# A recurrence and a bilinear feed-forward layer on one core: values loaded as 32-bit words, 512-column filling matmuls, sums of logarithms in place, and a new order of all work

## The chip, the cores and the metric

The kernel runs on one core of a Trainium2 chip. The metric is device time in microseconds (us) of one execution. Three executions of the kernel before took 206.62, 208.76 and 208.07 us, median 208.07 us. One further execution was profiled; it took 209.25 us, of which 207.3 us lie between its first and its last recorded instruction (the span).

Names of engines: PE is the matrix engine (PEld its weight loads), DVE the vector engine, ACT the scalar engine, POOL the general engine, SP the one that only issues transfers. Each works through its own list of instructions in order and waits on semaphores.

## The reference

Four sequences with eight heads, 768 steps, 48 elements per head. Each head holds a 48x48 state that decays by `alpha` and takes in an outer product; the result feeds a bilinear layer (3072 rows, 384 wide, 1536 hidden).

```python
for t in range(S):
    state = alpha[:, :, t, :, None] * state + np.einsum('bhd,bhe->bhde', k[:, :, t], v[:, :, t])
    y[:, :, t] = np.einsum('bhd,bhde->bhe', q[:, :, t], state)
x = y.transpose(0, 2, 1, 3).reshape(B * S, H * D)
out = ((x @ w_a) * (x @ w_b)) @ w_out
```

## The kernel before, in words

The steps are cut into six chunks: chunk c holds 256 steps (part c // 2 of the sequence) of two of the four sequences, u = 0 and 1. 128 partitions hold the 256 steps as neighbouring pairs, so each tile of inputs is `[128, 2 (u), 8 (heads), 2 (even and odd step), 48]`.

One chunk goes through two stages.

**Recurrence.** `ln` takes logarithms of alpha (ACT). `l2` adds the two steps of a pair (DVE). `A` (chunk 0, 32-bit matmul) or `H`, `L`, `A2` (chunks 1 to 5: the sum is split in two rounded parts, then two matmuls) multiply by a triangle of ones, which gives cumulative sums over pairs. `le` subtracts the odd step's logarithm to get the sum up to the even step. Four exponentials per u follow (`E`: b for the decay, i for its inverse, 0 for even and 1 for odd steps). `mk` and `mq` multiply keys and queries by them (DVE) into QKp. These are turned by PE and copied back (`C`, `Ce`, chunks 0 and 1) or turned by one transfer per u (`T`, chunks 2 to 5, issued by SP). `v` copies the values into a padded 16-bit tile. `D` makes scores for four heads (u, half), `M` masks them (DVE), `Y` multiplies them by the values, `SB` and `SA` add what the carried state gives, `X` copies the result from PSUM into xT. `K` and `k` bring the state forward; the decay of 64 pairs that they need comes from PE and ACT (`dk`, `de`) or by four small transfers through DRAM (`dec`).

**Feed-forward.** Hidden columns come in 12 blocks of 128. `a f` and `b f` are three matmuls each, either over both u (`*`, 512 columns) or over one (`0` or `1`, 256 columns); `as` copies the first product to SBUF (ACT), `pr` multiplies it by the second (DVE). `o m h` is six matmuls of 384 columns for 128 output rows, `ot` copies them out of PSUM, `st` stores them in two transfers on SP.

`ld` loads an input (chunks 0 and 1: each u by itself), `W` a slice of columns of w_a or w_b, `Wo` a half of w_out; the weights are rounded to 16 bit by the transfer, and so are the values in the kernel before, which takes POOL's queue. `warm n` issues n matmuls on zeros.

Nothing decides the order but a list written out by hand, PROGRAM (lines 17 to 425): each entry is a chunk and operations, issued in that order on the engine that each names. PSUM banks (0 to 7) are written into the list as well, so a matmul into a bank waits for whoever last read it. `gatet u` is a one-element POOL copy that holds POOL's list until the turned keys of u have landed; the next chunk's loads stand behind it.

The tiles la, l2, lh, ll and le exist once each, the input tiles twice.

Of the kernel before, what the change touches and what calls it, by code (L numbers as in the profile page):

```python
# [8 lines left out]
F32 = mybir.dt.float32  # L9
BF16 = mybir.dt.bfloat16  # L10
# [7 lines left out]
0: c1; warm 70 0; cz 0 V; cs 0 V  # L18
0: ld a 0 Y; ld k 0 Y; ld q 0 Y; ld a 1 Y; ld k 1 Y; cs 1 V; ld q 1 Y; gate a 0; ln 0; ld v 0 P; cm 0; cm 1; l2 0 V; A 0 1; warm 48 0; le 0; E 0 b1
0: E 0 i1; cz 1 V; W a 0 256; E 0 i0; W b 0 256; mk 0 V; ln 1; ld v 1 P  # L20
1: ld a 0 P
0: E 0 b0; l2 1 V
1: ld k 0 P
0: mq 0 V; A 1 0
1: ld q 0 P
0: warm 4 1; le 1; E 1 i1
1: ld v 0 P
0: C 0 0 1; dk 6; W a 256 768; E 1 b0; Ce 0 0 V; E 1 i0; W b 256 768; D 0 0 2; E 1 b1; v 0 V; warm 5 4; de; mk 1 V; W a 768 1536; C 0 1 0; K 0 6
0: W b 768 1536; Ce 0 1 S; mq 1 V; warm 11 1
1: ld a 1 P  # L30
0: k 0 0 V; C 1 0 4
1: ld k 1 P
0: M 0 0; SB 0 0
1: ld q 1 P
0: C 1 1 5; Ce 1 0 S
1: ld v 1 P
0: k 0 1 V; D 0 1 2; Ce 1 1 S; Wo 0 6; M 0 1; D 1 0 6; warm 16 4; Wo 6 12; v 1 S; M 1 0
2: ld a * P
0: K 1 4; Y 0; SA 0; k 1 0 V
2: ld k * P  # L40
0: SB 1 6; D 1 1 2; X 0 S; M 1 1
2: ld q * P
1: ln 0
0: a 1 0 0; a 0 0 1
2: ld v * P
0: k 1 1 V; as 1 0; Y 1; SA 1; b 1 0 5; X 1 S; pr 1 0; as 0 0
1: l2 0 V
0: a 5 0 2
1: H 0 S
0: a 3 0 4; as 5 0; a 4 1 5  # L50
1: L 0 V
0: b 0 0 1; as 3 0; a 4 0 6; pr 0 0; a 5 1 7; a 2 0 3; as 4 1; b 5 0 2; b 3 0 0; pr 5 0; b 4 1 4; pr 3 0; as 5 1; b 5 1 2; pr 4 1; as 4 0; b 4 0 7
0: a 2 1 1; as 2 0; pr 4 0; a 1 1 4; pr 5 1; b 2 1 0
1: A2 0 5
0: as 2 1; a 3 1 2
1: le 0; E 0 i1
0: b 3 1 7; b 2 0 6; as 1 1; pr 2 1; a 7 * 3
1: E 0 i0
0: pr 2 0; a 10 * 1; as 3 1
1: mk 0 V; E 0 b1  # L60
0: b 1 1 2; as 10 *; a 6 * 0; pr 3 1; pr 1 1
1: E 0 b0
0: a 0 1 5
1: v 0 V
0: as 7 *; b 11 * 4
1: mq 0 V
0: as 6 *; b 10 * 6; b 7 * 3
1: ln 1
0: pr 10 *; a 11 * 7; pr 7 *; as 0 1; b 6 * 0
1: l2 1 V  # L70
0: as 11 *
1: C 0 0 1
0: pr 6 *
1: H 1 S
0: a 9 * 3
1: Ce 0 0 S; L 1 V
0: b 0 1 2
1: dk 6
0: pr 11 *; as 9 *; pr 0 1
1: D 0 0 4  # L80
0: b 9 * 1
1: de; M 0 0; A2 1 7; C 0 1 6; E 1 i1
0: pr 9 *
1: K 0 2; E 1 b1
0: a 8 * 0
1: k 0 0 V; le 1
0: b 8 * 5
1: k 0 1 V; E 1 b0
0: o 3 0 1; as 8 *
1: mq 1 V; E 1 i0  # L90
0: o 0 0 3; pr 8 *
1: Ce 0 1 S
0: o 2 0 0
1: mk 1 V; SB 0 6; D 0 1 4; C 1 0 2; M 0 1
0: o 0 1 -; o 2 1 -; ot 0 S; o 3 1 -; ot 2 V
1: Ce 1 0 V
0: st 2 Y
1: Y 0; SA 0
0: ot 3 S
1: v 1 V; D 1 0 0  # L100
0: st 3 Y
1: K 1 4; X 0 S; M 1 0; C 1 1 3
2: ln *
1: b 3 0 2; a 1 0 6; Ce 1 1 V; b 11 0 1; a 3 0 0; k 1 0 V
0: o 1 0 7
1: as 3 0
2: l2 * V
1: as 1 0; b 1 0 0; k 1 1 V
0: o 1 1 -
2: H * S  # L110
1: pr 3 0; a 0 0 5; pr 1 0
0: ot 1 S
1: a 11 0 4
2: L * V
1: b 0 0 2; as 0 0; a 5 0 0; as 11 0; a 8 0 3; pr 0 0; as 5 0; SB 1 6; D 1 1 4; pr 11 0; as 8 0; a 4 0 0; M 1 1
2: A2 1 2
1: as 4 0
2: A2 0 1; E 1 i1
1: b 4 0 3; a 2 0 0
2: le 1; E 0 b1  # L120
1: b 5 0 4
2: le 0; E 1 b1
1: b 8 0 5; Y 1; SA 1
2: E 1 i0
1: pr 4 0
2: dec
1: pr 8 0
2: E 0 b0
1: pr 5 0; a 6 0 3; X 1 S
2: mk 1 V  # L130
1: a 7 0 2; a 10 0 5; as 2 0; b 11 1 7
2: mq 0 V; E 0 i1
1: b 2 0 4
0: st 1 Y
1: b 6 0 0; as 7 0; b 7 0 1; as 6 0; pr 2 0; a 9 0 6
2: E 1 b0
1: pr 7 0; a 2 1 3
0: st 0 Y
1: a 0 1 2; pr 6 0; as 10 0; b 10 0 4
2: mq 1 V  # L140
1: as 2 1; b 2 1 0; as 0 1; b 0 1 5
2: v 1 S
1: a 9 1 1; pr 10 0
2: T 1
1: b 9 1 2; pr 0 1; a 5 1 3; as 9 1; pr 2 1; a 4 1 4
2: E 0 i0
1: b 4 1 1; pr 9 1; as 4 1; b 5 1 5
2: mk 0 V
1: a 11 1 0; as 9 0; b 9 0 4; as 5 1; a 3 1 2; pr 4 1
2: T 0  # L150
1: b 3 1 6; pr 9 0; as 3 1; a 1 1 1; pr 5 1; a 8 1 3; as 11 1; b 1 1 4; pr 3 1; as 1 1; a 10 1 0; pr 11 1; as 8 1; b 8 1 6; pr 1 1
2: v 0 S; gatet 1; D 1 0 2
3: ld a * P
1: pr 8 1; a 7 1 1
2: M 1 0
1: as 10 1
2: K * 6
1: as 7 1
3: ld k * P
1: b 6 1 5  # L160
2: k * 0 V
1: a 6 1 3; b 7 1 4
3: ld q * P
1: as 6 1
2: D 0 0 0
1: o 3 0 2
2: k * 1 V
3: ld v * P
1: pr 7 1; b 10 1 6; o 2 0 3; pr 6 1; pr 10 1
2: M 0 0; SB 1 4; D 1 1 6  # L170
1: o 2 1 -
3: ln *
2: M 1 1
1: o 1 0 1; ot 2 S
3: l2 * V
2: Y 1; SA 1
3: H * V
1: o 1 1 -
2: X 1 S
3: L * V  # L180
2: SB 0 6
1: ot 1 S
2: D 0 1 4
1: o 0 0 3
2: M 0 1
1: st 1 Y
3: A2 0 0; A2 1 1; E 0 b1
2: Y 0; SA 0
3: le 1; E 0 i1; le 0; E 1 b1
1: o 3 1 -  # L190
2: X 0 V
3: E 0 i0; dec; E 1 i1
1: o 0 1 -
3: v 0 V; E 1 i0; mk 0 V; E 0 b0
2: a 4 * 7
3: E 1 b0; mq 0 V
2: a 3 * 0
1: st 2 Y
2: a 0 * 5; as 3 *
3: mq 1 V  # L200
2: b 3 * 6
3: T 0
2: as 4 *
3: mk 1 V
2: a 6 * 1
3: v 1 S
2: b 4 * 4; pr 3 *
1: ot 0 S
2: b 0 * 7; as 6 *
1: st 0 Y  # L210
2: pr 4 *; a 1 * 3; as 0 *; b 6 * 6
1: ot 3 S
2: pr 0 *
3: T 1
2: as 1 *; a 9 * 5
1: st 3 Y
2: pr 6 *; b 1 * 2; as 9 *
3: D 0 0 0
2: pr 1 *
3: K * 6; M 0 0  # L220
2: b 11 * 5; b 2 * 2
3: k * 0 V
2: a 11 * 1
3: gatet 1
2: a 2 * 0
4: ld a * P
2: as 11 *
3: k * 1 V
2: b 9 * 4; as 2 *
4: ld k * P  # L230
2: b 7 * 3; pr 9 *; a 7 * 1; pr 11 *
4: ld q * P
2: a 8 * 6; as 7 *; pr 2 *; a 5 * 0
4: ld v * P
2: as 8 *; pr 7 *
3: D 1 0 4
2: as 5 *; a 10 * 7
3: M 1 0
2: b 8 * 1; as 10 *; b 5 * 2; pr 8 *
4: ln *  # L240
3: SB 1 6
2: pr 5 *
3: D 1 1 4
2: b 10 * 0
3: M 1 1
2: o 0 0 2
4: l2 * V
2: o 3 0 3; pr 10 *
4: H * S
3: Y 1; SA 1  # L250
4: L * V
3: SB 0 4; D 0 1 0; X 1 S
2: o 0 1 -
3: M 0 1
4: A2 0 7
2: o 1 0 6; ot 0 V
4: E 0 b1; le 0
2: st 0 Y
3: Y 0; SA 0
4: E 0 b0  # L260
2: o 3 1 -
3: X 0 S
4: E 0 i1; A2 1 0
3: b 11 * 4
4: E 0 i0; le 1
3: a 0 * 2
2: ot 3 V
4: E 1 b0
3: a 11 * 5
4: mq 0 V  # L270
2: o 2 0 1
3: as 11 *
4: mk 0 V
3: as 0 *; b 0 * 3
4: T 0; E 1 i0
2: o 2 1 -
3: pr 0 *
4: E 1 i1; v 0 S; mk 1 V
2: o 1 1 -
4: E 1 b1  # L280
3: a 7 * 5
2: ot 2 S
4: mq 1 V
3: b 7 * 3
4: v 1 S
2: st 2 Y
3: pr 11 *; a 8 * 0
2: ot 1 S
3: a 5 * 1
4: T 1  # L290
3: as 7 *; b 8 * 2
4: dec
3: pr 7 *; as 5 *
4: D 0 0 6
3: a 3 * 5
4: M 0 0
3: a 2 * 1; as 3 *; b 5 * 3
2: st 1 Y
3: as 8 *; b 2 * 7; pr 5 *
2: st 3 Y  # L300
3: b 3 * 4; pr 8 *; as 2 *
4: gatet 1
5: ld a * P
3: a 1 * 6; pr 3 *; a 4 * 5; pr 2 *; as 1 *
5: ld k * P
3: b 1 * 4; as 4 *; b 4 * 2; pr 1 *
5: ld q * P
4: K * 6
3: pr 4 *; a 6 * 3
5: ld v * P  # L310
4: k * 0 V
3: b 6 * 1; as 6 *
4: D 1 0 4
3: pr 6 *
4: SB 1 2; D 1 1 6
3: a 10 * 0
4: M 1 0
3: a 9 * 1; as 10 *
4: M 1 1
3: b 10 * 5; as 9 *; b 9 * 4  # L320
5: ln *
3: o 2 0 1; pr 9 *; pr 10 *
4: SB 0 6; Y 1; SA 1
5: l2 * V
4: D 0 1 4
3: o 0 0 0
4: X 1 S; M 0 1
5: H * S
3: o 0 1 -
5: L * V  # L330
4: Y 0; SA 0
5: A2 1 2
4: X 0 S
3: o 2 1 -
5: le 1; E 1 i1
3: ot 0 V
4: a 4 * 7
5: E 1 i0; E 1 b0
4: b 6 * 6
5: mk 1 V; E 1 b1; A2 0 0  # L340
4: a 6 * 5
3: ot 2 V
5: E 0 b1
4: b 3 * 3
5: dec
4: as 6 *; a 3 * 1; as 4 *; pr 6 *; a 1 * 5; as 3 *
5: mq 1 V
4: b 4 * 6; as 1 *
5: le 0
4: b 1 * 1  # L350
5: T 1; E 0 i1
4: pr 4 *; a 7 * 2
5: E 0 i0
4: pr 3 *; a 0 * 5; as 7 *
5: mk 0 V
3: o 1 0 6
5: E 0 b0; v 0 S
4: pr 1 *; b 0 * 7; as 0 *
3: o 1 1 -
5: v 1 V; mq 0 V  # L360
4: a 5 * 1
3: ot 1 S
4: pr 0 *
5: T 0; K * 4
4: as 5 *
# [48 lines left out]
5: as 9 *; b 2 * 2; as 6 *; b 9 * 6; a 2 * 7; pr 9 *
4: o 2 0 4
# [13 lines left out]
def kernel(  # L429
# [11 lines left out]
    nc = tc.nc  # L441
# [479 lines left out]
```

## Time and profile before

| | before |
|---|---|
| median of three executions | 208.07 us |
| profiled execution, span | 209.25 us, 207.3 us |
| PE busy, matmuls | 192.6 us, 2702 |
| DVE, ACT, POOL busy | 139.9, 101.2, 38.0 us |
| first feed-forward matmul | 22.27 us |
| last matmul's start, last instruction | 202.66 us, 207.3 us |
| transfers | 29.42 MB, mean 142 GB/s |
| instruction queue q8 | 21 packets, 0.34 MB |

Times count from the span's start. A row of the page's fifth part gives a group of equal instructions: count, total busy time, mean duration, then the idle time of the engine before them and what ended it. Matmuls overlap in the pipeline, so a mean duration (379 ns for 512 columns) is longer than the distance between two starts. That distance, read from the start times in the trace where PE runs without a break, is 0.216 us for 512 columns, 0.109 us for 256, 0.163 us for 384 and 0.056 us for 128.

The page's second part cuts the span into 40 slices of 5.18 us; a digit is the busy share in tenths, and PEclk is the granted clock of PE. The trace also records transfers by queue; queue q8 brings PE's instructions in packets of 16,384 bytes, 256 instructions of 64 bytes.

### The profile page before, as it was taken

Reading aid. Unit: us, or ns where it says so; the run is one execution under the profiler, and the core shown is the slowest. Engines: PE = TensorE matmul, PEld = TensorE weight load, DVE = VectorE, ACT = ScalarE, POOL = GpSimd, SP = SyncE. Lnnn points to the kernel's source line nnn. Section 1 sums busy time; section 2 is a strip of 40 time slices with the busy share of each in tenths; the row PEclk is TensorE's granted clock in tenths of the full one; section 3 lists DMA queues with packets and bytes.
Section 4 is the critical chain, followed back from the end, with each engine's and each line's share of the span. In section 5 each row is a group of like instructions: output and inputs, shape, how many; then the busy total and the mean of one; then the engine's idle time right before and its main releaser. Section 6 shows DMA issues by size and latency. Waiting matters only on the chain.

```text
span 207.3 us, 6249 instructions
## 1 busy us (share of the span) xinstructions
PE 192.6 (93%) x2702; PEld 121.6 (59%) x2718; DVE 139.9 (67%) x223; ACT 101.2 (49%) x192; POOL 38.0 (18%) x54
## 2 busy tenths in 40 slices
PE   8988499999999989999998899999999999999991
PEld 8867378575778866564545554456545554454560
DVE  5799435887599979579885766698597755423530
ACT  3456344874378850567342576535683344332200
POOL 3896636000000027000080000530000000000000
PEclk9999859999999999999999999999999999999998
DMA  6999999999310697997959919699457200004155
GB/s 163 239 238 246 207 243 232 225 276 215 55 39 4 110 173 198 257 123 141 179 141 263 152 33 196 72 280 263 41 83 145 61 3 0 0 0 112 38 120 112
DMA packets 52587, 29.42 MB, mean 142 GB/s; under 512 B 42760, under 2 KB 49672, under 8 KB 52560
## 3 DMA queue, kind: packets, MB, share of 16 engines
q0 software_dynamic: 19552, 17.70, 45.5%
q1 hardware_dynamic: 33008, 11.33, 28.1%
q8 instruction: 21, 0.34, 0.6%
q14 instruction: 6, 0.05, 0.1%
HBM read 25.98 MB, written 4.74 MB: 148 GB/s over the span
## 4 chain that ended last, share of the span: by engine, by line
PE 53%; issue 24%; DMA 9%; DVE 6%; ACT 4%; POOL 2%; POOLq 0%; ACTq 0%; DVEq 0%
PE psum L789 28%; PE psum L812 15%; DMA a_t<-in_alpha_dram 7%; PE psum L738 4%; DMA kqT<-QKp 2%; ACT la L553 1%; DVE l L559 1%; PE psum L722 1%; PE psum L693 1%; ACT kqT L660 1%; PE psum L574 1%; PE psum L596 1%; DVE S L518 1%; DVE vx L513 1%; DVE m L727 1%
## 5 line engine op out<-in xcount | busy, mean ns | idle before, releaser
L789 PE MATMUL psum<-xT,wa_t 128*128 128x512 bf16 (+1 forms) x262 | 57.2, 344 | 1.3 <-ACT xT L773 0.6
L789 PE MATMUL psum<-xT,wb_t 128*128 128x512 bf16 (+1 forms) x262 | 56.4, 338 | 0.6 <-issue 0.5
L812 PE MATMUL psum<-wo_t,prod 128*128 128x384 bf16 x288 | 51.5, 326 | 0.1
L812 PEld LDWEIGHTS <-prod 128*128 128x128 bf16 x288 | 27.2, 98 | 19.3 <-issue 0.3
L789 PEld LDWEIGHTS <-wa_t 128*128 128x128 bf16 x270 | 26.2, 101 | 20.4 <-issue 0.9
L789 PEld LDWEIGHTS <-wb_t 128*128 128x128 bf16 x270 | 25.8, 99 | 19.9 <-issue 0.3
L727 DVE TENSOR_TENSOR m<-psum,mask 128x1024 bf16<-128x1024 f32 x24 | 29.0, 1220 | 7.9 <-PE psum L722 7.7
L839 POOL CAST go<-kqT 1x1 f32<-1x1 bf16 x3 | 0.5, 173 | 83.9 <-DMA kqT<-QKp 83.9
L773 ACT ACTIVATE xT<-psum 128x768 bf16<-128x768 f32 x11 | 8.9, 808 | 14.4 <-PE psum L738 14.3
L817 ACT ACTIVATE ot<-psum 128x384 f32<-128x384 f32 x13 | 6.4, 492 | 18.2 <-PE psum L812 18.2
L553 ACT ACTIVATE la<-a_t 128x768 f32<-128x768 f32 (+1 forms) x8 | 9.3, 1165 | 11.6 <-DMA a_t<-in_alpha_dram 11.6
L738 PE MATMUL psum<-m,vx 64*64 64x128 bf16 x576 | 10.9, 221 | 2.8 <-issue 2.5
L722 PE MATMUL psum<-kqT 64*64 64x128 bf16 x384 | 10.3, 219 | 2.7 <-DVE prod L802 1.7
L738 PEld LDWEIGHTS <-vx 64*64 64x64 bf16 x576 | 8.9, 109 | 6.1 <-issue 6.1
L570 PE MATMUL psum<-wz 128*128 128x128 bf16 x154 | 11.2, 238 | 1.0 <-DVE one L493 1.0
L614 DVE TENSOR_TENSOR QKp<-k_t,invb 128x768 bf16<-128x768 f32 x12 | 11.4, 953 | 0.9 <-ACT invb L610 0.9
L570 PEld LDWEIGHTS <-wz 128*128 128x128 bf16 x154 | 10.3, 108 | 1.9 <-DVE one L493 1.0
L614 DVE TENSOR_TENSOR QKp<-q_t,beta 128x768 bf16<-128x768 f32 x12 | 11.3, 951 | 0.0
L722 PEld LDWEIGHTS <-kqT 64*64 64x64 bf16 x384 | 7.2, 106 | 5.3 <-issue 3.8
L819 DVE COPY ot<-psum 128x384 f32<-128x384 f32 x11 | 6.0, 553 | 6.0 <-PE psum L812 6.0
L601 DVE TENSOR_TENSOR le<-psum,la 128x384 f32<-128x384 f32 x12 | 6.5, 553 | 5.0 <-PE psum L596 3.7
L559 DVE TENSOR_TENSOR l<-la 128x384 f32<-128x384 f32 (+1 forms) x8 | 6.0, 746 | 4.7 <-ACT la L553 4.7
(244 smaller groups left out, 261.3 us busy)
## 6 DMA issues: line engine op xcount, KB each, us to landing
out_dram<-ot SPq DMA_DIRECT2D x48, 96.0 KB, 2.2
a_t<-in_alpha_dram POOLq DMA_DIRECT2D x4, 768.0 KB, 7.8
k_t<-in_k_dram POOLq DMA_DIRECT2D x4, 768.0 KB, 9.7
q_t<-in_q_dram POOLq DMA_DIRECT2D x4, 768.0 KB, 11.4
v_t<-in_v_dram POOLq DMA_DIRECT2D x4, 384.0 KB, 12.4
wo_t<-in_moe_w_out_dram POOLq DMA_DIRECT2D x2, 576.0 KB, 16.0
a_t<-in_alpha_dram SPq DMA_DIRECT2D x2, 384.0 KB
k_t<-in_k_dram SPq DMA_DIRECT2D x2, 384.0 KB, 6.9
```

Of the source, the lines that this page charges most:

```text
L553: nc.scalar.activation(out=ch.la[:, us].rearrange("p b h r d -> p (b h r d)"), in_=ch.a[:, us].rearrange("p b h r d -> p (b h r d)"), func ...
L559: eng.tensor_add(ch.l2[:, us].rearrange("p b h d -> p (b h) d"), x[:, :, 0, :], x[:, :, 1, :])
L570: nc.tensor.matmul(w[:, :C], lhsT=wz, rhs=wz, start=True, stop=True)
L601: nc.vector.tensor_sub(ch.le[:, u], ch.pf[u].rearrange("p (h d) -> p h d", h=H), ch.la[:, u, :, 1, :])
L614: eng.tensor_mul(QKp[ch.c % 2][:, u, j, :, :, :D], src[:, u].rearrange("p h r d -> p r h d"), by[:, :, u])
L722: nc.tensor.matmul(s2[g * HC:(g + 1) * HC, r, p, rk, :], lhsT=ch.kqT[u][rs, 1, rk, 2 * h + p, g * HC:(g + 1) * HC], rhs=queriesT(ch, u, 2 ...
L727: nc.vector.tensor_mul(m.rearrange("p r a k s -> p (r a) (k s)"), ch.s2[u, h].rearrange("p r a k s -> p (r a) (k s)"), maskn(4))
L738: nc.tensor.matmul(y[c * DP:(c + 1) * DP, g, j // 2 * C:(j // 2 + 1) * C], lhsT=lhsT, rhs=rhs, start=(g, c) not in begun, stop=False, skip ...
L773: nc.scalar.activation(out=o_, in_=i_, func=AF.Copy)
L789: nc.tensor.matmul(p, lhsT=(wa_t, wb_t)[w][:, kk, f * 128:(f + 1) * 128], rhs=ch.xT[:, kk, us, :], start=(kk == 0), stop=(kk == KT - 1))
L812: nc.tensor.matmul(op, lhsT=ch.prod[:, f, m * C:(m + 1) * C], rhs=wo_t[:, f, :], start=(f == 0), stop=(f == NFF - 1))
L817: nc.scalar.activation(out=ot, in_=ch.pf["o", m], func=AF.Copy)
```

## The change

Values stay 32-bit words when they are loaded, so that a load of values may stand on SP's queue; the copy `v` does the rounding. Filling matmuls have 512 columns instead of 128, and there are 37 of them instead of 154 (17 instead of 70 in the first group). Weights come in slices of 256, 768 and 512 columns instead of 256, 512 and 768. The tiles l2 and le are gone: from chunk 1 on the sums of pairs overwrite the even half of la, and `le` later overwrites them in the same place; chunk 0 uses lh and ll for them. Chunk 1's decay goes through DRAM instead of PE. The clearing of the state tiles moves from DVE to POOL. All loads and all operations of PROGRAM stand in a new order, with other banks and in places other engines; chunk 0 makes four of its twelve hidden blocks in halves instead of six.

```diff
-0: c1; warm 70 0; cz 0 V; cs 0 V
-0: ld a 0 Y; ld k 0 Y; ld q 0 Y; ld a 1 Y; ld k 1 Y; cs 1 V; ld q 1 Y; gate a 0; ln 0; ld v 0 P; cm 0; cm 1; l2 0 V; A 0 1; warm 48 0; le 0; E 0 b1
-0: E 0 i1; cz 1 V; W a 0 256; E 0 i0; W b 0 256; mk 0 V; ln 1; ld v 1 P
+0: c1; warm 17 0; cs 0 P; cz 0 V
+0: ld a 0 Y; ld a 1 Y; ld v 0 Y; ld k 0 Y; cm 0; cm 1; ln 0; l2 0 V; ld q 0 P; ln 1; A 0 1; ld k 1 P; warm 3 0; ld q 1 P; l2 1 V; E 0 i1; cs 1 P
+0: E 0 b1; le 0; A 1 7; E 0 b0; dk 0; le 1; E 1 b1; ld v 1 P; v 0 V; E 0 i0; warm 6 2
 1: ld a 0 P
-0: E 0 b0; l2 1 V
+0: E 1 i0; W b 0 256; mk 0 V; E 1 i1; de; W a 0 256; mq 0 V; E 1 b0; K 0 2; warm 2 4
+1: ld a 1 P
+0: C 0 0 0; mk 1 V; W a 256 1024; warm 4 1; Ce 0 0 S; W b 256 1024; k 0 0 V; mq 1 V; W b 1024 1536; D 0 0 6; C 0 1 4; W a 1024 1536; k 0 1 V
+0: C 1 0 5; v 1 S
+1: ld q 0 P
+0: M 0 0; warm 2 0
 1: ld k 0 P
...
+0: Ce 1 0 S; K 1 0
+1: ld k 1 P
+0: warm 1 2; k 1 0 V; Ce 0 1 S
+1: ld q 1 P
+0: D 1 0 6; k 1 1 V; C 1 1 3; Wo 0 6; M 1 0; SB 0 4; Ce 1 1 S; D 0 1 0
 1: ld v 0 P
...
+0: warm 2 2; Wo 6 12
+1: ln 0
+0: M 0 1; SB 1 6; D 1 1 2
 1: ld v 1 P
...
+0: M 1 1
 2: ld a * P
...
+0: Y 0; SA 0
 2: ld k * P
...
+0: X 0 S
+1: l2 0 V
+0: Y 1; SA 1
+1: H 0 S
+0: a 1 0 5
 2: ld q * P
-1: ln 0
-0: a 1 0 0; a 0 0 1
+0: X 1 V
+1: ln 1
+0: b 1 0 3; a 0 0 0; b 0 0 1
+1: L 0 V
 2: ld v * P
...
-    wz = cst.tile([C, C], BF16, name="wz")
+    wz = cst.tile([C, 512], BF16, name="wz")
...
-            setattr(ch, what, ld.tile([C, 2, H, 2, D], BF16 if what == "v" else F32, name=what + "_t"))
+            setattr(ch, what, ld.tile([C, 2, H, 2, D], F32, name=what + "_t"))
...
+    def part(ch, name, dtype):
+        if not hasattr(ch, name):
+            setattr(ch, name, wk.tile([C, 2, H, D], dtype, name=name, bufs=1))
+        return getattr(ch, name)
+
+    def sums(ch):
+
+        return part(ch, "lh", F32) if ch.c == 0 else ch.la[:, :, :, 0, :]
+
     def pairs(ch, us, eng):
-        if not hasattr(ch, "l2"):
-            ch.l2 = wk.tile([C, 2, H, D], F32, name="l2", bufs=1)
         x = ch.la[:, us].rearrange("p b h r d -> p (b h) r d")
-        eng.tensor_add(ch.l2[:, us].rearrange("p b h d -> p (b h) d"), x[:, :, 0, :], x[:, :, 1, :])
+        eng.tensor_add(sums(ch)[:, us].rearrange("p b h d -> p (b h) d"), x[:, :, 0, :], x[:, :, 1, :])
...
-            nc.tensor.matmul(w[:, :C], lhsT=wz, rhs=wz, start=True, stop=True)
+            nc.tensor.matmul(w, lhsT=wz[:, :C], rhs=wz, start=True, stop=True)
...
+    def evens(ch):
+        return part(ch, "ll", F32) if ch.c == 0 else ch.la[:, :, :, 0, :]
+
     def even(ch, u):
-        if not hasattr(ch, "le"):
-            ch.le = wk.tile([C, 2, H, D], F32, name="le", bufs=1)
-        nc.vector.tensor_sub(ch.le[:, u], ch.pf[u].rearrange("p (h d) -> p h d", h=H), ch.la[:, u, :, 1, :])
+        nc.vector.tensor_sub(evens(ch)[:, u], ch.pf[u].rearrange("p (h d) -> p h d", h=H), ch.la[:, u, :, 1, :])
```

`high`, `low`, `cum`, `expo` and `decay_pe` read the sums and the even parts through the new helpers and do the same arithmetic. The lists of chunks 1 to 5 are rewritten throughout. Of the old list the prediction also uses this place (`gatet 1` stands some lines ahead of it):

```
4: ln *
3: SB 1 6
2: pr 5 *
3: D 1 1 4
2: b 10 * 0
3: M 1 1
2: o 0 0 2
4: l2 * V
2: o 3 0 3; pr 10 *
...
3: SB 0 4; D 0 1 0; X 1 S
```

In the new list the same steps of chunks 3 and 4 read `3: D 1 0 6; K * 2` to `4: ln *`, `4: l2 * V`, `3: SB 0 6; D 0 1 4`, with more matmuls of chunk 2 between `gatet` and `l2`; and chunk 1 has `E 1 i1; dec` where the old list has `dk 6` and `de`.

## The prediction

> **What bounds the kernel now.** I read the slices of the page first. The second part of the page, rows PE, POOL, clock and transfers:
>
> ```profile
> PE   8988499999999989999998899999999999999991
> ...
> POOL 3896636000000027000080000530000000000000
> PEclk9999859999999999999999999999999999999998
> DMA  6999999999310697997959919699457200004155
> ```
>
> PE is full almost everywhere from the sixth slice (25.9 us) on. The weak place is the fifth and sixth: a 4 in PE, then an 8 and a 5 in its clock. The stretches 18 to 31.6 us by themselves (columns: length, busy time and instructions of PE, PEld, DVE, ACT, POOL, then granted clock, share of transfers, GB/s):
>
> ```profile
> 18.00:21.40 3.40, 2.73 (x138) 2.46 (x128) 2.67 (x4) 1.37 (x2) 1.78 (x2) 1.00 1.37 214
> 21.40:24.80 3.40, 1.54 (x46) 1.05 (x35) 1.85 (x3) 1.81 (x3) 1.95 (x4) 1.00 1.25 208
> 24.80:28.20 3.40, 2.13 (x34) 1.65 (x35) 0.10 (x1) 0.92 (x2) 1.47 (x2) 0.50 1.17 209
> 28.20:31.60 3.40, 3.40 (x18) 2.35 (x16) 1.77 (x4) 1.62 (x5) 1.17 (x1) 0.50 1.12 272
> ```
>
> After a stretch with PE 45% busy the clock is granted at half for two stretches, and comes back after one that was full. The chain of waits names what emptied it (start, length, what):
>
> ```profile
> 19.70 0.45 issue
> 20.15 0.34 PE psum L693 x19
> ...
> 23.08 0.51 PE psum L738 x25
> 23.59 2.48 issue
> 26.07 1.17 PE psum L738 x28
> 27.24 5.22 PE psum L789 x27
> ```
>
> Two gaps wait for nothing that the profile shows. Counting PE's instructions in program order (each 32-bit matmul is four), the first gap stands before instruction 704 and the second before 960, 256 apart, which is one packet of queue q8. That queue's packets start at 10.75, 17.56, 23.75 and 29.65 us, and PE resumes 1.3 to 1.4 us after the second and third end (18.82 to 20.15, 24.70 to 26.07). I take both gaps as PE out of instructions: it used 256 (short 64-row matmuls) faster than a busy transfer system brought them, about 6 us from one block's use to the next one's arrival (20.15 to 26.07).
>
> [...]
>
> **Part by part.** *Start of the feed-forward.* Before: first matmul of it 22.27 us, and by 32.46 us 36 matmuls of 256 columns (6 before the gap, the others mostly at half clock). After, from rows of this trace: a load of 0.39 MB lands every 1.5 us on SP's queue (alpha 4.64, then 6.14, 7.65, 9.15), so alpha u1, values u0, keys u0 land at 6.1, 7.7, 9.2. POOL first clears state tiles. POOL fills of that size aren't in the trace: at least 0.3 us (its 64x256 fill), at most 1.7 us by the slope from 64 to 256 elements (145 to 320 ns); I take 2.5 us for the pair, the slope, because the list has them unpacked. Its 8 mask steps take 2.6 us, so queries u0 are issued at 7.0 and then keys and queries u1; 3 us to the first packet (issue 8.99, packets 11.8 for weights) and 1.5 us each give landings of 11.9, 13.4, 14.9. A second clearing delays values u1 to a landing near 17. From there by rows: `mq` 11.9, 0.95 us; `C 0 0`; `mq` of u1 at 14.9; `v 1` on ACT 17.1 to 17.95 (845 ns); `K 1`; then `Ce 1 0`, `Ce 0 1`, `Ce 1 1` of 1.02 us each to 21; `M 1 0`, `M 0 1`, `M 1 1` of 1.22 us from 19.5 to 23.2; `Y 0`, `Y 1` of 0.9 us. Without a gap the feed-forward would start at 24.4. The new list reaches it after 771 instructions instead of 897 (37 filling matmuls, not 154), so the block limit at 960 lies after it; only 704 lies in a fast stretch, inside `Y 1`. Its block is asked for when 448 is crossed, just before `C 1 1` near 18.2, and 6 us later is 24.2 against 23.5 when it is wanted: a gap of 0.7 us. Start 25.2, with no recurrence of chunk 0 left. 36 matmuls at 0.109 us end at 29.1 instead of 32.46: **-3.3 us** if the clock stays. Each microsecond by which values u1 land later moves it one to one.
>
> *Weights.* They land by the trace's rates (1.0 us for 256 columns, 2.9 for 768, 1.9 for 512, behind those loads) at 20 to 21, 25.4, 28.3, 30.2, 32.1 us. `a 5` wants the second at 26.5, `b 2 1` the third at 29.3, `b 11` the fourth at 32.5: cover of about 1 us, nothing added. If it goes, PE waits one to one.
>
> *Values as words.* A half of the values took 0.9 us of transfers (landings 21.54 and 22.46), alpha 1.5: +0.6 each, 2.4 us over four halves, before chunk 2's alpha, which I put at 50 us against its use (`ln`) at 53. Hidden with 3 us. On ACT the copy has 845 ns for 16-bit values and I change nothing; on DVE it lies between 351 ns (16-bit row) and 957 ns (128x768 cast from PSUM), four copies, at most 2.4 us of an engine 67% busy: 0.
>
> [...]
>
> *Sums in place.* DVE's sum of 384 elements takes 537 ns, of 768 954 ns; the same work with another stride. New wait: `ln` of the next chunk has to follow the exponentials that read the even part. In the list they are at least 9 us earlier. Price 0; if the strided access were slower by as much as the even exponential is against the odd (518 to 488 ns), 40 such steps cost 1.2 us of ACT and DVE, not of PE.
>
> *Chunk 1's decay.* PE loses 64 records: they took from 43.46 to 44.20, **-0.7 us**. The four transfers on SP stand 10 us ahead of `k`, behind nothing but stores' list.
>
> *Halves.* 24 halves become 12 wholes: 24 x 0.109 = 2.62 against 12 x 0.216 = 2.59. 0. Moving `X`, `ot`, clearing between DVE and ACT: both below 70%, 0; `X` on DVE is 957 against 808 ns, at most 0.15 us on the path each time.
>
> *Chunks 2 to 5.* Here PE waited at 75.2, 86.2, 88.7 and 112.9 us, 0.8, 0.5, 0.5 and 1.9 us. The last, in the timeline (start, length, engine, line, operation, idle before):
>
> ```profile
> 103.12 0.17 POOL L839 CAST go<-kqT 1x1 f32<-1x1 bf16 x1 [21.65 <-DMA kqT<-QKp]
> ...
> 111.74 1.48 ACT L553 ACTIVATE la<-a_t 128x1536 f32<-128x1536 f32 x1 [3.59 <-DMA a_t<-in_alpha_dram]
> ...
> 113.25 0.96 DVE L559 TENSOR_TENSOR l<-la 128x768 f32<-128x768 f32 x1 [2.52 <-ACT la L553]
> ...
> 114.13 0.68 DVE L802 TENSOR_TENSOR prod<-as__2165,psum 128x512 bf16<-128x512 bf16 x1
> ...
> 114.86 0.42 PE L722 MATMUL psum<-kqT 64*64 64x128 bf16 x16 [1.71 <-DVE prod L802]
> ```
>
> DVE sits on the pair sum until alpha has landed behind the gate; the product behind it holds PE's bank. Adding PE's work by the distances in the table, from gate to pair sum: 7.5, 8.4, 10.2 us before (chunks 3, 4, 5), 6.4, 9.9, 8.9 after. From a turn to its first use, chunk 2: 4.6 before (it waited 0.8), 5.6 after. So chunk 4 gains about 1.5, chunk 2 0.8, chunk 3 loses about 1.1: -1.2 on balance, of which I take half, **-0.6**, since banks and DVE's neighbours changed too. Ends: -3.8 (all four gone) to +6 (three such waits of 2 us more).
>
> *End.* The last `o`, `ot` and `st` are the same kind: 0.
>
> Sum: 209.25 - 3.3 - 0.7 - 0.6 = 204.65, so **204.7 us**. The profiled execution lies 1.2 us above the median 208.07; the four times shown spread over 2.6 us, about what the half clock costs (5.6 us of work at half, 2.8 us), so the runs may differ in it.
>
> **Rivals.** *Half clock again.* The new list has fewer fillers late: between 14.5 and 17.9 PE has one `D` (0.42 us), two `C` (0.61 each) and two fillers (0.43), 2.1 of 3.4 us or 60%. If the clock is halved as the feed-forward starts, up to 2.8 us go: 207.5. For: 63% at half clock did not bring it back. Against: 80% kept it. 0.25.
>
> *The fetch gap stays whole* (the change doesn't do what it seems to): `Y 1` waits 2 us more, 206.7. 0.07.
>
> *Slower: DVE stuck on alpha.* The mechanism just shown, in the three pair sums after a gate. For: 6.4 us in chunk 3 against 0.2 + 0.5 + 7.2 for gate, issue and landing plus 1.5 for the logarithms, 9.4 us. Loads of words add to the queue. With 2 us for each of three chunks, and 0.7 of the start's gain lost to values u1: 204.7 + 6 + 0.7 = 211.4. It decides once alpha lands over 10 us after its issue instead of 7.2 to 7.6. Against: turns come earlier than before. 0.23.
>
> **Numbers.** Forecast 204.7 with 0.45 (203 to 206). About 1% is what a measurement can tell from no change: 206.0 to 210.1. The first rival is within it, the second too. Chances: faster 0.50, same 0.26, slower 0.24. Range 202.3 to 210.9: low end with all four waits gone and half a microsecond less clearing, high end into the slower rival.
>
> **What will show it.** The first feed-forward matmul at 24.4 to 26 us; at most one gap without cause, before PE instruction 704, under 1 us; full clock from 26 us; alpha of chunk 2 landed by 51 us; no DVE wait over 2.5 us on logarithms. Wrong if values u1 land after 18 us, if the clock is half past 28 us, or if PE waits in chunks 2 to 4 sum to more than 4 us.

## The result: 237 us instead of 208

The changed kernel takes 237.07 us (median of four executions, 234.51 to 239.48); the kernel before takes 208.41 us beside it (four, 206.62 to 209.17). The ratio is 1.130, 95% interval 1.116 to 1.145; it goes by the two faster executions of the changed kernel alone (234.51 and 236.06), and the profiled one is one of the two slower. The forecast was 204.7 us with a range up to 210.9: wrong, and on the other side.

The profiled execution of the changed kernel took 239.48 us, its span is 236.7 us. From the first and second part of its page:

```profile
span 236.7 us, 5851 instructions
...
PE   7968899920999998999100299999999999999992
...
PEclk9997999995699999999955589999999999999999
DMA  7999999996021799749999700849905656102105
```

A slice is now 5.92 us. The 4 that PE had in its fifth slice before is gone, but PE has two holes that were not there: a 2 and a 0 (47 to 59 us), and 1 0 0 2 (112 to 136 us). Within each hole the clock falls to half, and it stays there from 52.6 to 62.9 us and from 117.5 to 138.0 us. PE works again from 59.6 and from 134.6 us, so only some 3.3 us of work behind each hole run at half clock: an estimate of 1.7 us lost each time. The view of waits (engine and line, what they wait for, total us, times, longest) names both:

```profile
PE psum L734 <- DMA kqT<-QKp: 21.4, 1, 21.4
...
DVE Sm L719 <- DMA bl<-row: 11.1, 1, 11.1
...
PE psum L750 <- DVE Sm L719: 10.5, 1, 10.5
```

Each is one single wait. Chunk 1's carried-state matmuls (L750) wait for `k`, which waits for `bl`, the decay that now comes through DRAM. Chunk 3's scores (L734) wait for `T 0`, the turn of its keys and queries. Neither transfer is issued late. Before, all transfers of the same kinds landed soon after their issue. The views by tile of the kernel before give, for `bl` and then for the turns:

```profile
DMA to landing us min/median/max: 2.0/2.4/2.7
...
DMA to landing us min/median/max: 4.3/4.3/4.4
```

The first place in the timeline of the changed kernel (start, length, engine, line, operation, idle before):

```profile
34.11 1.15 POOL L553 DMA_DIRECT2D a_t<-in_alpha_dram  x1 [0.46 <-DMA k_t<-in_k_dram]
34.68 0.59 SPq L631 DMA_DIRECT2D row<-beta  x2
...
38.36 1.15 POOL L553 DMA_DIRECT2D v_t<-in_v_dram  x1
39.51 0.91 SPq L634 DMA_DIRECT2D bl<-row  x2
...
59.19 0.36 DVE L719 TENSOR_TENSOR Sm<-psum,bl 128x192 bf16<-128x192 f32 x1 [11.11 <-DMA bl<-row]
...
59.60 0.53 PE L750 MATMUL psum<-kqT,Sm 64*64 64x128 bf16 x6 [10.48 <-DVE Sm L719]
```

`bl` is issued in two transfers, at 39.51 and 39.88; the second lands 19.2 us after its issue. Between issue and landing chunk 2's four loads (issued 34.11 to 39.5) are on the way. `bl` consists of 1536 packets of four bytes; the loads' packets mostly have 4224 bytes and take 252 ns each. From 44 to 54 us the records show 672 of the former and 567 of the latter, near one for one, and the small ones speed up when the large ones thin out (483 against 35 in 56 to 58 us). A four-byte packet itself takes 13 ns, which makes 20 us for 1536 one after the other and 1.2 us spread over the page's 16 engines. That `bl` spends the rest of its 19.2 us waiting behind large packets is an estimate from these counts. The last of the small ones starts at 58.5 us, the last packet of the loads at 58.3. The prediction had not weighed such a mixture.

The second place:

```profile
100.84 1.79 SPq L677 DMA_TRANSPOSE kqT<-QKp  x1
102.74 1.14 SPq L631 DMA_DIRECT2D row<-beta  x2
105.24 0.17 POOL L851 CAST go<-kqT 1x1 f32<-1x1 bf16 x1 [17.08 <-DMA kqT<-QKp]
105.39 0.90 SPq L634 DMA_DIRECT2D bl<-row  x2
105.88 1.16 POOL L553 DMA_DIRECT2D a_t<-in_alpha_dram  x1 [0.47 <-ACT ot L829]
106.39 13.35 SPq L677 DMA_TRANSPOSE kqT<-QKp  x1
...
134.59 0.64 PE L734 MATMUL psum<-kqT 64*64 64x128 bf16 x16 [21.40 <-DMA kqT<-QKp]
```

The new list has chunk 3's turns in the order `T 1; dec; ... T 0`, then `gatet 1`. The gate names the turn of u 1, which is the first of the two. So the gate opens at 105.24, chunk 4's loads start at 105.88, and the second turn is issued at 106.39, after them. The first turn of the same chunk took 4.3 us. The second stands in the chain of waits (start, length, what) of the kernel before with the first of these lines, in that of the changed kernel with the second:

```profile
98.58 4.42 DMA kqT<-QKp
...
106.39 28.15 DMA kqT<-QKp
```

Its 2048 packets of 256 bytes took 73 ns in the mean instead of 21. Here the mixture is not one for one: from 109 to 134 us there are 729 packets of the loads beside the 2048. So the account of the first place does not carry over as it stands; why the turn is slow among loads is not shown, only that it is.

**Where the time went.** The table takes the moment at which PE has done a given amount of its work (all matmuls but the fillers, counted in PE time at full clock, 168 us in all; read from the starts of the weight loads, which the trace holds without gaps) and gives the distance to the kernel before in us. Rows below "changed" are the experiments. Each row is one profiled execution; up to the feed-forward they are all one program, and still its first matmul came at 25.3 to 26.9 us.

| work done, us of PE (kernel before is there at) | 26 (49.7) | 32 (56.6) | 74 (102.4) | 80 (109.1) | 164 (197.8) |
|---|---|---|---|---|---|
| changed | -3.9 | +8.2 | +8.0 | +31.1 | +29.7 |
| decay on PE again | -1.9 | -1.7 | -1.7 | +19.9 | +19.8 |
| gate on the last turn | -2.6 | +9.5 | +9.7 | +15.1 | +15.3 |
| loads held behind `bl` | -0.3 | -0.4 | -0.9 | +20.0 | +18.2 |
| both repairs | -2.2 | -1.9 | -0.7 | +3.5 | +5.1 |
| both, alpha ahead of the gates | -2.6 | -2.4 | -3.4 | -3.7 | -1.9 |

The changed kernel is 3.9 us ahead when chunk 0's work is well under way (the forecast had 3.3). Then it loses 12.1 us at the decay and 23.1 us at the turn, and nothing more.

### The profile page after: what moved, and what is told of

It reads as the page before. It is cut to its first block, busy times and chain, and to the rows that moved or that the text cites. A ratio compares the mean times of both kernels' runs of the same rounds, so it can differ in the third digit from the quotient of the medians.

```text
span 236.7 us, 5851 instructions
## 1 busy us (share of the span) xinstructions
PE 192.5 (81%) x2504; PEld 113.7 (48%) x2525; DVE 138.2 (58%) x212; ACT 103.6 (44%) x193; POOL 43.9 (19%) x59
## 4 chain that ended last, share of the span: by engine, by line
PE 40%; DMA 26%; issue 21%; POOL 9%; ACT 1%; DVE 0%; POOLq 0%; ACTq 0%
PE psum L801 20%; PE psum L824 14%; DMA kqT<-QKp 14%; DMA q_t<-in_q_dram 7%; DMA a_t<-in_alpha_dram 6%; PE psum L750 3%; POOL S L526 1%; POOL q_t L553 1%; PE psum L734 1%; POOL k_t L553 1%; POOL wa_t L536 1%; POOL wb_t L536 1%; PE psum L607 1%; POOL v_t L553 1%; POOL a_t L553 1%
## 5 line engine op out<-in xcount | busy, mean ns | idle before, releaser
L801 PE MATMUL psum<-xT,wa_t 128*128 128x512 bf16 (+1 forms) x256 | 56.3, 343 | 0.9 <-ACT as__1451 L807 0.5
L824 PE MATMUL psum<-wo_t,prod 128*128 128x384 bf16 x288 | 52.8, 331 | 1.0 <-ACT ot L829 0.9
L801 PEld LDWEIGHTS <-wa_t 128*128 128x128 bf16 x264 | 25.2, 99 | 21.2 <-issue 2.7
L801 PEld LDWEIGHTS <-wb_t 128*128 128x128 bf16 x264 | 25.1, 98 | 20.8 <-issue 1.3
L734 PE MATMUL psum<-kqT 64*64 64x128 bf16 x384 | 11.6, 234 | 22.3 <-DMA kqT<-QKp 21.4
L829 ACT ACTIVATE ot<-psum 128x384 f32<-128x384 f32 x18 | 8.4, 487 | 27.7 <-PE psum L824 27.6
L734 PEld LDWEIGHTS <-kqT 64*64 64x64 bf16 x384 | 8.0, 114 | 25.4 <-DMA kqT<-QKp 21.9
L750 PE MATMUL psum<-kqT,Sm 64*64 64x128 bf16 x144 | 8.7, 227 | 10.5 <-DVE Sm L719 10.5
L750 PEld LDWEIGHTS <-Sm 64*64 64x64 bf16 x144 | 5.3, 110 | 15.0 <-DVE Sm L719 10.9
L585 PE MATMUL psum<-wz 128*128 128x512 bf16 x34 | 10.9, 457 | 1.4 <-DVE one L501 1.2
L750 PE MATMUL psum<-m,vx 64*64 64x128 bf16 x576 | 10.5, 218 | 1.2 <-issue 0.6
L750 PEld LDWEIGHTS <-vx 64*64 64x64 bf16 x576 | 8.7, 107 | 3.5 <-issue 3.5
L719 DVE TENSOR_TENSOR Sm<-psum,bl 128x192 bf16<-128x192 f32 x4 | 1.4, 356 | 13.4 <-DMA bl<-row 11.1
L785 ACT ACTIVATE xT<-psum 128x768 bf16<-128x768 f32 x8 | 6.5, 807 | 4.6 <-PE psum L750 4.6
```

The lines of the kernel that those rows point to most:

```text
L585: nc.tensor.matmul(w, lhsT=wz[:, :C], rhs=wz, start=True, stop=True)
L734: nc.tensor.matmul(s2[g * HC:(g + 1) * HC, r, p, rk, :], lhsT=ch.kqT[u][rs, 1, rk, 2 * h + p, g * HC:(g + 1) * HC], rhs=queriesT(ch, u, 2 ...
L750: nc.tensor.matmul(y[c * DP:(c + 1) * DP, g, j // 2 * C:(j // 2 + 1) * C], lhsT=lhsT, rhs=rhs, start=(g, c) not in begun, stop=False, skip ...
L785: nc.scalar.activation(out=o_, in_=i_, func=AF.Copy)
L801: nc.tensor.matmul(p, lhsT=(wa_t, wb_t)[w][:, kk, f * 128:(f + 1) * 128], rhs=ch.xT[:, kk, us, :], start=(kk == 0), stop=(kk == KT - 1))
L824: nc.tensor.matmul(op, lhsT=ch.prod[:, f, m * C:(m + 1) * C], rhs=wo_t[:, f, :], start=(f == 0), stop=(f == NFF - 1))
```

## Experiments

Line numbers move by a few from kernel to kernel. "Before" beside each group is the old kernel on the same chip: 209.28 us (median of 7; the first four runs), 209.48 (13; `gateb`, the gate in the old list, and alpha ahead in both kernels) and 209.27 (17; the rest). Runs of different groups are best compared by their ratios to it.

**1. Undo each suspect alone, then both.** The theory is two separate crossings, that is, transfers of small packets that are on the way at the same time as loads; the rival for each is that the new order of feed-forward work holds the loss.

Decay on PE again (`dk`, `de` in place of `dec`):

```diff
-1: le 0
+1: dk 4; le 0
...
-0: cz 1 V; as 6 *; b 2 1 6
+0: cz 1 V
+1: de
+0: as 6 *; b 2 1 6
...
-1: E 1 i1; dec
+1: E 1 i1
```

> The changed kernel, with chunk 1's decay made by PE and ACT again (as in the kernel before) instead of four small transfers through DRAM. Theory (the small transfers crossed chunk 2's loads): the wait of 10.5 us in chunk 1 goes, with the half clock after it (1.6 us of work), and PE gets 0.7 us of its own back: 237 - 11.4, so 225 to 226 us; the wait of 21 us in chunk 3 stays. Rival (chunk 1's state was late for another reason, the sums in place or the late values): the wait stays and the time is 237 to 238.

Measured 229.66 us (ratio 1.095, 1.086 to 1.105). The hole at 49 to 60 us is gone and the other is untouched (table). It came out some 4 us above the expectation. Half of that is there by 49.7 us, where the kernel is 1.9 us ahead instead of 3.9: the banks that the decay holds make a feed-forward group wait 1.40 us, and PE's gap at the start lasted 1.15 us instead of 0.64 (part 5). The other half is not accounted for.

Gate on the last turn:

```diff
-3: gatet 1
+3: gatet 0
```

> The changed kernel with one word changed: in chunk 3 the gate waits for the turned keys of u 0, the turn that is issued last, not of u 1. Theory (the last turn crossed chunk 4's loads): it lands in 4.3 to 4.6 us again, the wait of 21.4 us and 1.7 us of half clock go, chunk 4's alpha comes 5 us later and costs up to 2 us: 214 to 216 us. Rival (the turn was slow by itself or waited for the decay's transfers ahead of it on SP's queue): it still takes over 20 us, and the time is 236 or more.

Measured 223.92 us (1.068, 1.060 to 1.076). One digit gives back 13 us, 8 us less than expected. The same turn, still behind the decay's transfers on SP's list but ahead of the loads, is quick again in the chain of waits:

```profile
108.02 5.94 DMA kqT<-QKp
```

So it was not slow by itself or by the decay ahead of it. Of the 23.1 us at this place 5.4 are left (table, from +9.7 to +15.1): all loads now start later, at 114.73, and alpha is late.

Both:

> The changed kernel with both repairs (chunk 1's decay by PE, chunk 3's gate on the last turn). If the two crossings are all that went wrong, what the prediction summed up for the rest stands: 237 - 11.4 - 22 gives 203.6, the prediction had 204.7 with its own 0.7 for the decay on PE not to be had (205.4): 203 to 206 us, 1 to 2.5% under the kernel before. If something else in the new order is worse, over 208.

Measured 214.87 us (1.022, 1.011 to 1.032). That is 22.2 us of the 28.7 that were lost, so the two crossings are the bulk; but it is 9 us above the upper end of what was expected, and still above the kernel before. What it waits for then, in DVE's timeline:

```profile
83.72 0.96 DVE L576 TENSOR_TENSOR la<-la 128x768 f32<-128x768 f32 x1 [3.34 <-ACT la L563]
...
111.86 0.96 DVE L576 TENSOR_TENSOR la<-la 128x768 f32<-128x768 f32 x1 [4.83 <-ACT la L563]
```

These are the pair sums of chunks 3 and 4, waiting for logarithms and so for alpha behind the gate: the prediction's slower rival, smaller than the crossings and hidden behind them in the changed kernel.

**2. Is it the crossing, or the way through DRAM?** Chunk 3's `dec` behind its second turn, the gate as changed:

```diff
-3: dec; E 0 b0; v 0 V
+3: E 0 b0; v 0 V
...
-3: T 0
+3: T 0; dec
```

> The changed kernel with chunk 3's decay transfers moved behind its last turn on SP's queue, the gate left on u 1. If the turn was late because it stood behind the decay's wait for its row (SP was held to 106.3 us though the queries were multiplied by 104.8), the turn goes out 1.5 us earlier, is mostly done when the loads' first packets come (108.2 us), and 15 to 23 us go: 214 to 222. If only the gate matters, the tail of the turn still crosses the loads and less than 10 us go: over 227.

Measured 229.01 us (1.092, 1.084 to 1.100). By its size that is the second expectation; the timeline shows neither:

```profile
100.47 5.33 SPq L677 DMA_TRANSPOSE kqT<-QKp  x2
104.85 0.17 POOL L851 CAST go<-kqT 1x1 f32<-1x1 bf16 x1 [16.36 <-DMA kqT<-QKp]
105.49 1.16 POOL L553 DMA_DIRECT2D a_t<-in_alpha_dram  x1 [0.47 <-ACT ot L829]
105.89 1.82 SPq L631 DMA_DIRECT2D row<-beta  x2
...
111.95 0.96 SPq L634 DMA_DIRECT2D bl<-row  x2
...
123.59 0.56 DVE L723 TENSOR_TENSOR Sm<-tmp,bl 128x384 bf16<-128x384 f32 x1 [14.22 <-DMA bl<-row]
```

Both turns now go out ahead of the loads, the second 1.0 us ahead (at 104.48), and are quick: all eight turns of this kernel take 4.3 to 4.4 us. The decay goes out 0.4 us behind the first load and takes the turn's place as the victim: the row needs 4.93 us, `bl` 11.13, DVE waits 14.2 us. In the changed kernel and in this one the small transfer that is issued after the first load is the late one (the turn 28.15 us, `bl` 11.13).

The other way round: the decay of chunk 1 stays in DRAM, and chunk 2's loads wait for it.

```diff
-2: ld a * P
...
-2: ld k * P
...
-2: ld q * P
...
-2: ld v * P
...
-1: E 1 i1; dec
+1: E 1 i1; dec; gateb
+2: ld a * P; ld k * P; ld q * P; ld v * P
...
+    def gate_b(x):
+        nc.gpsimd.tensor_copy(go, bls[x.c % 2][0:1, 0, 0:1])
```

> The changed kernel, chunk 1's decay still through DRAM, but chunk 2's four loads are issued by POOL only after a one-element copy of bl, so that no load is on the way beside row and bl. Theory 'crossing' (the 1536 four-byte packets of bl queue one for one with the loads' packets): bl lands 2 to 3 us after its issue, as in the kernel before, instead of 19.2; the wait of DVE at Sm goes and with it about 10 us, 226 to 230 us in all, as when PE made the decay (229.66); chunk 3's loss stays. Rival 'the way through DRAM is slow there by itself': bl still lands late, 235 us or more. If the held loads are then late for chunk 2, a new wait on chunk 2's alpha shows after 60 us.

Measured 223.79 us (1.068, 1.056 to 1.080).

```profile
43.04 0.90 SPq L631 DMA_DIRECT2D bl<-row  x2
46.65 0.18 POOL L852 COPY go<-bl 1x1 f32<-1x1 f32 x1 [12.97 <-DVE prod L814]
47.28 1.15 POOL L550 DMA_DIRECT2D a_t<-in_alpha_dram  x1 [0.46 <-issue]
...
51.56 0.35 DVE L716 TENSOR_TENSOR Sm<-psum,bl 128x192 bf16<-128x192 f32 x1
```

With no load of chunk 2 beside it `bl` has landed 3.6 us after its issue, and DVE's wait is gone. So the way through DRAM was not slow by itself here. The time is 2 us below the range that was expected. It came out 6 us under the kernel with the decay on PE; at 80 us of work the two profiles stand level (+20.0 and +19.9), and its four executions spread over 6.4 us, so I leave that difference open.

**3. The same in the kernel before.** If the crossing is what costs, the old kernel must suffer it too once its order lets the two meet. First the gate's word alone:

```diff
-3: gatet 1
+3: gatet 0
```

> The kernel before with one word changed: chunk 3's gate waits for the turn of u 0, which is the first of its two turns, so that chunk 4's loads are issued before or beside the turn of u 1. Theory 'a turn that meets the loads takes 10 to 28 us': T 1 of chunk 3 takes over 10 us instead of about 4.5, PE waits for its scores, 214 to 230 us. Rival 'the loss belongs to the new order of the FF work, the gate alone costs nothing': 206 to 210 us.

Measured 206.44 us (0.989, 0.981 to 0.997): no loss at all, against the expectation. In the old list the second turn goes out right behind the first:

```profile
98.81 2.07 SPq L665 DMA_TRANSPOSE kqT<-QKp  x1
99.51 0.18 POOL L839 CAST go<-kqT 1x1 f32<-1x1 bf16 x1 [18.27 <-DMA kqT<-QKp]
100.52 1.17 POOL L545 DMA_DIRECT2D a_t<-in_alpha_dram  x1 [0.83 <-issue]
```

It is issued 1.7 us before the first load and takes 4.4 us. With the other turn on the way before the loads, the gate on the wrong turn cost nothing here. The same gate, and the decay put between the two turns, so that its round trip holds the second one:

```diff
-3: E 0 i0; dec; E 1 i1
+3: E 0 i0; E 1 i1
...
-3: T 0
+3: T 0; dec
...
-3: gatet 1
+3: gatet 0
```

> The kernel before, chunk 3's gate on its first turn and chunk 3's decay moved on SP's list from before the first turn to right behind it, so that the row's round trip holds the second turn back by some 3 us, until chunk 4's loads are on the way. With the gate alone moved, the second turn was issued 1.7 us before the first load and took 4.3 us (206.44). Theory 'it is not the word of the gate, it is a turn issued after the first load': the second turn takes over 8 us, PE waits for it at chunk 3's scores, 212 to 230 us. Rival 'the 28 us turn of the changed kernel has a cause of its own': the turn stays under 6 us, 205 to 208 us.

Measured 221.19 and 225.23 us, against 209.27 of the kernel before.

```profile
99.84 0.90 SPq L622 DMA_DIRECT2D bl<-row  x2
100.71 1.17 POOL L545 DMA_DIRECT2D a_t<-in_alpha_dram  x1 [0.83 <-ACT as__2000 L795]
...
102.18 13.43 SPq L665 DMA_TRANSPOSE kqT<-QKp  x1
...
122.72 0.64 PE L722 MATMUL psum<-kqT 64*64 64x128 bf16 x16 [15.83 <-DMA kqT<-QKp]
```

Issued 1.5 us after the first load instead of 1.7 before it, the turn takes 20.49 us instead of 4.4, PE waits 15.8 us, and the clock falls to half in that wait (from 109.1 to 126.2 us). The hole of the changed kernel stands in the old one, with the old order of feed-forward work. Three traces of the changed kernel and its variants have the late turn too: issued 0.5 to 0.6 us behind the first load it took 28.15 us in the changed kernel, 25.83 with the decay on PE, 25.23 with the loads held behind `bl`.

**4. What is left: alpha.** In the repaired kernel, alpha of chunks 3, 4 and 5 is loaded ahead of the gate, right behind the chunk before it (and `b 5` moves from bank 5, which the decay holds, to bank 3):

```diff
 2: ld v * P
+3: ld a * P
...
-3: ld a * P
...
 3: ld v * P
+4: ld a * P
```

and so on for chunk 5.

> The changed kernel with both repairs (chunk 1's decay on PE, chunk 3's gate on the last turn), alpha of chunks 3, 4 and 5 loaded ahead of the gates, and one FF matmul group (b 5) moved off the bank that the decay holds. Theory 'what is left of the loss, 6 us over the kernel before, is alpha that comes late behind the gates of chunks 3 and 4': 204 to 208 us. Rival 'the rest is something else (the order of FF work, the clock)': 212 to 216 us, as with the repairs alone (214.87).

Measured 208.48 us (ten executions; 0.998, 0.992 to 1.003). 6.4 us go (5 us by the two ratios), and the changed order is level with the old one, 0.5 us above what was expected. The moved bank is in this run too, and was not measured apart: the group `b 5` waited 1.40 us for it. The table shows the kernel 3.7 us ahead at 109 us and 1.9 at the end; between them PE waits 1.72 us for chunk 4's second turn, at 124.66, and 1.18 us without a cause, at 137.48 (part 5). The same move in the old kernel:

> The kernel before with the alpha loads of chunks 3, 4 and 5 moved ahead of the gates, right behind the four loads of the chunk before (chunk 3's behind chunk 1's last logarithms, since they share a buffer). Theory: PE's and DVE's waits on alpha in chunks 3 to 5 (some 3 us together) go, 203 to 207 us. Rival: the alpha load meets the decay or the turn of the chunk before it, a turn takes over 8 us: 210 us or more. Third: the waits were hidden, 207 to 209 us.

Measured 205.98 us (0.985, 0.976 to 0.994): faster than the kernel before, and by its ratio than the repaired kernel, though the two intervals touch. The waits of its logarithms on alpha (ACT) fall from 11.6 us in four to 2.6 us in one, that of the start.

**5. The fillers and the block limit.** The gain at the start was forecast from PE running out of instructions at limits of 256. The repaired kernel of part 4 with its 37 wide fillers as 148 narrow ones, the same PE time by the distances of before (4 x 0.056 us beside 0.216) in 111 matmuls more:

```diff
-            nc.tensor.matmul(w, lhsT=wz[:, :C], rhs=wz, start=True, stop=True)
+            nc.tensor.matmul(w[:, :C], lhsT=wz[:, :C], rhs=wz[:, :C], start=True, stop=True)
```

(and each count times four).

> The repaired changed kernel with alpha loaded ahead (208.48 us), its 37 filling matmuls of 512 columns as 148 of 128 columns: 111 matmuls more, the same time of PE. Theory 'out of instructions': the border that it crosses with a gap of 0.48 us moves ahead, and another border, with 1.5 to 3 us, comes to stand before the FF work; the first FF matmul comes 1 to 3 us later, 209 to 212 us. Rival: no change, 207 to 209 us.

Measured 214.33 us (1.026, 1.017 to 1.034), 5.9 us more than with wide fillers. PE's timeline has three gaps with no cause ahead of the feed-forward where there was one of 0.48 us:

```profile
16.04 0.90 PE L587 MATMUL psum<-wz 128*128 128x128 bf16 x13 [0.99 <-issue]
...
22.24 0.30 PE L736 MATMUL psum<-kqT 64*64 64x128 bf16 x7 [1.42 <-issue]
...
28.16 0.53 PE L752 MATMUL psum<-m,vx 64*64 64x128 bf16 x11 [1.57 <-issue]
```

They sum to 3.98 us; the feed-forward starts at 28.94 instead of 25.54 us, and runs at half clock up to 34.21. A start 3.40 us later, and half of 5.27 us, make 6.0 us: that accounts for the 5.9 us. It is more than the 1 to 3 us expected, which left out the clock.

The old kernel with wide fillers only (154 narrow ones become 39 wide):

> The kernel before with its filling matmuls alone changed: a quarter as many, of 512 columns instead of 128. Theory 'PE runs out of instructions at each border of 256': some 230 of PE's instructions fewer stand ahead of the FF work, so the border that cost 2.48 us falls into FF work, where 256 instructions last over 25 us, and the gap and the half clock behind it go; a gap of 0.3 to 1 us is left at the border before; 204 to 207 us. Rival 'the 2.48 us belong to that place in the program': the gap stays before the same matmul, 207 to 210 us.

Measured 207.56 us (twelve executions; 0.996, 0.992 to 1.000). The gap did not go:

```profile
20.59 0.60 PE L570 MATMUL psum<-wz 128*128 128x512 bf16 x2 [1.12 <-issue]
...
26.50 0.80 PE L738 MATMUL psum<-m,vx 64*64 64x128 bf16 x36 [2.08 <-issue]
```

The expectation had an error in its counting: 230 instructions fewer are nearly one block, so the limit of before's instruction 704 comes to stand about where 960 stood. By itself this gap could belong to its place in the program, as the rival said. What decides is the count of instructions. PE has a weight load and a matmul by turns, so 128 weight loads stand for 256 instructions. Queue q8 has 21 packets in the kernel before for 2702 matmuls and 2718 weight loads, 258 instructions a packet; by its start times one comes every 126 weight loads in the mean, in the kernel before and in the changed one. The gaps stand ahead of weight loads 352 and 480 in the kernel before, 352 in the changed and the repaired kernel, 224 and 352 here, and 224, 352 and 480 with narrow fillers. These are different matmuls (carried state, scores, fillers, `Y`), but always a multiple of 128 apart. All fourteen traces together hold 26 gaps of over 0.35 us without a cause, and each stands ahead of weight load 224, 352, 480, 864, 2016 or 2144. Each also ends 2.25 to 2.90 us after a packet of q8 starts: before 2.59 us (17.56 to 20.15) and 2.32 (23.75 to 26.07), changed 2.35 (22.72 to 25.07), the repaired kernel 2.36 (22.49 to 24.85) and, at weight load 2016 in the middle of the program, 2.63 (134.85 to 137.48). By these numbers PE does stand still for its instructions, and the rival is out.

Last, the old kernel with alpha ahead and wide fillers together:

> The kernel before with alpha loaded ahead of the gates (205.98 us) and the wide filling matmuls. If both gains stand (waits on alpha, the gap of 2.48 us), 202 to 205 us, below both kernels; if the wide fillers bring nothing, 205 to 207 us.

Measured 204.52 us (six executions, 203.58 to 206.50; 0.984, 0.976 to 0.991), the fastest version here and below both kernels. Beside alpha alone (0.985) the fillers bring nothing that can be told apart.

## Why the prediction was wrong, step by step

*Start of the feed-forward: right.* The forecast was a start at 25.2 us, one gap of 0.7 us inside `Y 1`, 3.3 us gained. The first feed-forward matmul came at 25.76, and the gap is there:

```profile
25.07 0.58 PE L750 MATMUL psum<-m,vx 64*64 64x128 bf16 x28 [0.64 <-issue]
...
25.76 0.50 PE L801 MATMUL psum<-xT,wa_t 128*128 128x256 bf16 x3
```

It stands ahead of weight load 352, which is instruction 704. At equal work the changed kernel is 2.5 to 3.9 us ahead from 36 to 50 us. That the size of the gap fits (0.64 us for 0.7) is in part luck: in the six other traces with the same program up to here (parts 1, 2 and 4) the same gap lasted 0.37 to 2.31 us, and the start came at 25.34 to 26.88. The pieces held too: the two pairs of clearings on POOL took 2.3 and 2.6 us for the 2.5 assumed; the copy of values u1 began at 16.8 us for a landing "near 17". Two sums of the prediction do not come out as written, without effect on the rest: issue at 7.0, 3 us and 1.5 us make 11.5 for the queries, not 11.9 (they were multiplied from 11.44), and the low end as described would be about 201, not 202.3.

*Half clock again: half right.* The clock fell to half at 18.5, after a stretch of 3.4 us with PE 39% busy where too few fillers were feared, but came back at 21.9, before the feed-forward. In two of the six other traces with the same start the half clock did come as the feed-forward began (24.8 to 28.2 us and 25.1 to 32.0), and in these two the gap at instruction 704 was longest, 1.45 and 2.31 us.

*Weights, values as words, sums in place, halves: right.* No matmul waited for a weight. The copy of 32-bit values took 553 ns on DVE (bounds 351 and 957) and 839 on ACT (845 before), the sums 550 to 559 and 955 ns (537 and 954 before).

*Chunk 1's decay: the first failure.* The step reads "The four transfers on SP stand 10 us ahead of `k`, behind nothing but stores' list", and takes 0.7 us off. The distance was there: the row was issued at 34.68, and DVE was ready for `bl` at 48.1. What failed is that the transfers were put at nothing because of SP's list. Chunk 2's four loads of 768 KB, which POOL had issued, were on the way beside them, and row and `bl` together took over 24 us (34.68 to 59.07). In place of -0.7 stands +12.1 us. The step priced the transfers by the rows of before, in which this crossing does not occur: there every decay through DRAM goes out ahead of the next loads (the closest, chunk 4's, at 131.56 against 132.07).

*Chunks 2 to 5: the second failure.* The step compared distances from gate to alpha and from turn to use, and took -0.6. It never put the second turn beside the gate. The new list shows it: `T 1; dec`, then `T 0`, then `gatet 1`, with SP held by `dec` until its row is back (102.74 to 106.29). In place of -0.6 stand 23.1 us. The mechanism is no wait on alpha. In the old list the second turn of a chunk is issued 4.1 to 5.6 us ahead of the next chunk's first load (72.82 and 76.88, 98.58 and 104.13, 126.78 and 132.07 us); in the new one chunk 3's is issued 0.5 us behind it.

*The slower rival, DVE on alpha: real, but not this.* It was priced at 6 us; in the repaired kernel loading alpha ahead, with the moved bank, gave 5 to 6.4 us back. In the changed kernel it is covered by the holes.

So the sum would have been 204.7 + 12.8 + 23.7 = 241 us with the two terms as measured, against 239.48 profiled.

What stays open: why a turn is slow among loads at all, its packets not alternating with theirs one for one, and why it took 28 us in one order and 20 in another; and the 6 us between the held loads and the decay on PE.

## What to carry to other kernels

In these kernels a transfer of many small packets (a scatter of single words, a turn by transfer) was quick when it was on the way before the bulk loads (in the kernel before `bl` 2.0 to 2.7 us, a turn 4.3 to 4.4) and late when it was issued after the first of them (`bl` 11.1 to 19.2 us, a turn 20.5 to 28.2): issue it before them, or hold them back. For the scatter the counts (672 of its packets beside 567 large ones in 10 us) put the price on the large packets among its own and not on its bytes, 6 KB; that is an estimate. For the turn the cause is open, the price as high. When an order is written anew, read for every gate what it keeps apart, and check that it names the last of the guarded transfers, not the first. Price a transfer from a row in which the same neighbours are on the way; where no such row exists, the life of the neighbours is an estimate: in the changed kernel chunk 2's loads lasted 24.2 us (34.11 to 58.3) and row and `bl` 24.4 (34.68 to 59.07), chunk 4's loads 27.8 us (105.88 to 133.7) and the turn 28.15. And count instructions: a border of 256 in a stretch of short matmuls cost 0.4 to 2.5 us here, and the half clock behind it, where it came, 1.7 to 3.4 us more (an estimate: half of 3.4 to 6.8 us).

## What was not expected of the hardware

- Small packets and large ones from two queues alternated near one for one (672 to 567 in 10 us): `bl` 19.2 us instead of 2.4.
- A turn by transfer among loads took 20.5 to 28.2 us in four traces instead of 4.3 to 4.4, and beside it, from 110 to 134 us in the changed kernel, all transfers together moved 64 to 241 GB/s in stretches of 3 us, against up to 276 in a slice of the same run.
- A start some 1.5 us earlier or later against the loads made the difference here: 1.0 us ahead of the first load the turn takes 4.3 to 4.4 us, 0.5 us behind it 25 to 28.
- PE stood still for instructions 26 times in fourteen traces, 0.37 to 2.48 us each, always at a limit of 256 instructions; but not at every limit.
- Each hole costs again in the clock: some 3.3 us of work at half speed behind each of the two in the changed kernel.
